# A threshold attention followed by a mixture of attention experts: the opening's loads reordered, and the first pair of heads computed one head at a time

## The chip, the core and the metric

One core of a Trainium2 chip. The metric is the device time of the whole program in microseconds (us), the median over runs. Engines: PE (TensorE, matmuls and transposes), DVE (VectorE), ACT (ScalarE), POOL (GpSimd) and SP (SyncE, which here only issues DMAs). ACT issues DMAs too. PE writes its results to PSUM, eight banks of 512 fp32 columns in 128 partitions; DVE and ACT read them from there.

## The reference

Two stages, in fp32, for batch 8. First an attention with 8 heads, 576 tokens and head size 64, in which only scores within `tau` of their row's maximum count; then, on its output `x` (576 tokens by 512), a mixture of 4 causal attention experts of head size 64, of which each token takes the two with the largest gate.

```python
scores = q @ k.T / sqrt(64)
scores = where(scores >= max(scores) - tau, scores, -1e9)
attn = exp(scores - max(scores)); attn /= sum(attn) + 1e-9
x = attn @ v                              # heads side by side
logits = x @ w_gate                       # top 2 of 4, softmax over them: w
for e in range(4):
    a = softmax(causal(x @ wq[e] @ (x @ wk[e]).T / sqrt(64)))
    out += chosen(e) * w(e) * (a @ (x @ wv[e]) @ wo[e])
```

## The kernel before

The unit of the first stage is a pair of heads: 32 pairs, `pair(n)` for n from 0 to 31, four to a batch. The two heads of a pair lie in partitions 0 to 63 and 64 to 127. `prep(n)` loads the pair and transposes it; 512 of the 576 tokens go as four blocks of 128 (tiles s = 0 to 3), the last 64 tokens of both heads together are a fifth tile (s = 4), loaded into a tile `tm` ("tails": keys and queries). `scores(n, s, qk)` makes a tile: the score matmuls into PSUM (two halves of 288 columns for each head), then for each head DVE's row maximum (`reduce`), POOL's threshold (`thr`), ACT's exponential (`exp`), DVE's masked product with the row sum (`stt`), DVE's addition and reciprocal of the sums (`inverse`), and POOL's multiplication by them (`scaled` on `pp`). `transp` transposes the normalised rows by PE and copies them by ACT, `transp_tails` does it for the last 64 columns, `attnv` multiplies by the values. After the four pairs of a batch, `moe(b)` does the second stage (`projected`, `values`, `scores2`, `transp2`, `attnv2`, `output`), its work mixed with that of the next batch's pairs. Its weights are loaded and split in two parts during the opening (`load_weights`: ACT copies, POOL subtracts).

Pairs 0 and 1 (`DIRECT = 2`) open the kernel, and `first(n)` prepares them without the split into two parts that later pairs have: keys into `ki`, queries into `qi` (in the trace they are `pt`, after the buffer that they use), PE transposes them, ACT copies the keys into `kx` (a `p2` buffer, in the trace `p`), DVE scales the queries into `qx`. Pair 0's tail queries `qd` use an `st` buffer, pair 1's a `pt2t` buffer. In `scores`, the four matmuls of a tile of these pairs (two heads by two halves) are issued with the heads in turn, on partitions 0 to 63 and 64 to 127, and their two bank pairs are taken as one group (`both[-1].v.first = both[0].v`). Each such fp32 matmul is two instructions in the trace: 16 of them are two tiles of two heads.

No engine's order follows the program text. Every operation becomes an `Op` of a `Plan` with a place: a base (the pair, or a number below zero for the opening) plus the number that `PLACE` has for its unit (`"tT"`, or `"tT@0"` for base 0 alone), plus `PLACE_OP` for its engine and tile. `arrange()` runs through planned time: each engine takes, of what is ready by the planned costs and for which buffers are free, what has the smallest sum; PE may start at most `AHEAD = 3` groups beyond the first that is not yet started in its own sorted line. The result is one fixed order on each engine. Every engine's queue, and SP's and ACT's DMA issues in it, is served in that order on the chip; an instruction that waits holds back all behind it. `fill()` puts matmuls with the constant tile `still` into the gaps that the plan shows on PE in the first 80 us; they keep TensorE's clock up and compute nothing that is used. All helpers record their operations in a few lines: L584 a matmul, L1264 a transpose (and every later `fn` of the plan), L1261 a `still` matmul, L605 ACT's copy, L612 a memset, L634 `scaled`, L642 `reduce`, L645 the reciprocal, L656 `stt`, L672 `exp`, L684 a load.

Of the kernel before, what the change touches and what calls it, by code (L numbers as in the profile page):

```python
# [69 lines left out]
}  # L70
# [17 lines left out]
}  # L88
AV_GROUPS = ((4, 0, 1), (2, 3))
AHEAD = 3  # L90
DIRECT = 2
AV2_GROUPS = ((4, 3), (2, 1, 0))
AV2_AT = (((1, "av1"), (2, "av0")), ((2, "av1"), (3, "av1")))

# [1200 lines left out]
```

## Time and profile before

| | |
|---|---|
| median of 3 runs | 924.8 us (924.16 to 925.0) |
| the profiled execution | 924.31 us, of which the span from the first to the last instruction is 922.6 us |
| granted TensorE clock, mean over the span | 0.996 of 2.4 GHz |
| busy share of the span | PE 97%, DVE 80%, ACT 71%, POOL 48% |

Busy shares are means over the span, and PE's contains the `still` matmuls. The rows of a timeline tell when an instruction began, how long it and those merged with it took, how long its engine had been idle before, and what released it.

### The profile page before, as it was taken

To read this page: it belongs to the slowest core of one execution; us is meant where nothing else is said; L and a number is where in the kernel's file an instruction comes from. 1 tells how busy PE (TensorE), PEld (TensorE's weight loads), DVE (VectorE), ACT (ScalarE), POOL (GpSimd) and SP (SyncE) were. 2 spreads that over 40 slices of the span, in tenths; PEclk is the share of its full clock that TensorE was granted. 3 is DMA by queue.
4 is the path that set the end of the run, shared out by engine and by line. 5 is a ranking of instruction groups with operands and counts; after the bars stand their busy time and mean duration, and the time that the engine had idled before them with its cause. 6 is when DMAs were issued, how large, how long until landed. Compare 5 with 4: busy or idle time off the path is not lost.

```text
span 922.6 us, 26089 instructions
## 1 busy us (share of the span) xinstructions
PE 899.3 (97%) x9261; PEld 838.2 (91%) x9261; DVE 736.8 (80%) x2142; ACT 652.4 (71%) x1540; POOL 438.5 (48%) x899
## 2 busy tenths in 40 slices
PE   6899999999999999999999999999999999999996
PEld 5678999899999999999999999999999999999985
DVE  4888879887788869888698877988778886988275
ACT  3678758886778757887587865888677875787453
POOL 4776435554356534555255643555435653444100
PEclk9999999999999999999999999999999999999999
DMA  6544654653755545755437555474474555560151
GB/s 133 143 119 105 154 128 107 159 132 97 173 130 138 140 113 137 178 137 131 120 96 185 125 125 143 116 176 121 102 176 120 145 137 124 123 166 27 50 124 58
DMA packets 147506, 117.86 MB, mean 128 GB/s; under 512 B 98992, under 2 KB 107184, under 8 KB 147376
## 3 DMA queue, kind: packets, MB, share of 16 engines
q1 hardware_dynamic: 144832, 115.61, 51.0%
q8 instruction: 73, 1.20, 0.6%
q10 hardware_dynamic: 2544, 0.59, 0.4%
q14 instruction: 57, 0.47, 0.2%
HBM read 30.42 MB, written 9.44 MB: 43 GB/s over the span
## 4 chain that ended last, share of the span: by engine, by line
PE 86%; DVE 5%; DMA 2%; ACT 2%; POOL 2%; SPq 2%; issue 1%; POOLq 0%; DVEq 0%; ACTq 0%
PE banks L584 64%; PE banks L1264 22%; DVE pp L656 2%; SPq L682 1%; POOL pp L634 1%; ACT pp L672 1%; DVE col L642 1%; DVE banks L661 1%; ACT pt L605 1%; DMA tm<-in_k_dram 1%; SPq L684 1%; DMA pt<-in_k_dram 1%; DVE col L632 0%; DMA st<-in_moe_wq_dram 0%; DMA kt<-hl 0%
## 5 line engine op out<-in xcount | busy, mean ns | idle before, releaser
L634 POOL TENSOR_SCALAR pp<-pp,col 128x576 f32<-128x576 f32 x288 | 212.9, 748 | 177.4 <-DVE col L645 140.3
L642 DVE TENSOR_REDUCE col<-banks 128x1 f32<-128x576 f32 x304 | 226.5, 751 | 35.0 <-PE banks L584 30.8
L656 DVE SCALAR_TENSOR_TENSOR pp<-banks,col,pp 128x576 f32<-128x576 f32 x288 | 231.0, 813 | 29.0 <-ACT pp L672 19.6
L605 ACT ACTIVATE pt<-banks 128x512 f32<-128x512 f32 (+2 forms) x400 | 224.0, 588 | 39.1 <-PE banks L1264 36.6
L672 ACT ACTIVATE pp<-banks,col 128x576 f32<-128x576 f32 (+1 forms) x298 | 217.0, 738 | 42.5 <-DVE col L642 38.0
L1264 PE MATMUL banks<-ident,pp 128*128 128x128 f32 x1342 | 195.7, 275 | 3.3 <-POOL pp L634 1.6
L584 PE MATMUL banks<-kt,qt 128*128 128x288 f32 x960 | 175.3, 311 | 0.9 <-DMA kt<-hl 0.3
L1264 PEld LDWEIGHTS banks<-ident,pp 128*128 128x128 f32 x1342 | 156.5, 141 | 15.0 <-issue 4.1
L634 POOL TENSOR_SCALAR col<-col,tau_n 128x1 f32<-128x1 f32 x288 | 76.7, 268 | 193.5 <-DVE col L642 147.1
L584 PE MATMUL banks<-pt,vm 128*64 128x128 f32 (+1 forms) x2560 | 154.8, 264 | 0.0
L584 PEld LDWEIGHTS banks<-kt,qt 128*128 128x128 f32 x960 | 135.2, 189 | 6.7 <-issue 3.6
L584 PEld LDWEIGHTS banks<-pt,vm 128*64 128x64 f32 x2560 | 131.1, 137 | 8.4 <-issue 4.5
L672 ACT ACTIVATE p<-banks,col 128x576 f32<-128x576 f32 (+4 forms) x134 | 73.2, 553 | 26.3 <-DVE col L661 13.0
L605 ACT ACTIVATE x<-banks 128x256 fp32r<-128x256 f32 (+1 forms) x96 | 28.4, 329 | 73.8 <-PE banks L584 73.7
L634 POOL TENSOR_SCALAR p<-p,col,gw 128x384 f32<-128x384 f32 (+3 forms) x112 | 67.4, 611 | 12.1 <-DVE col L645 6.8
L584 PE MATMUL banks<-wvh,x 128*128 128x260 f32 x320 | 64.3, 285 | 0.0
L661 DVE CUSTOM_DVE_ANT_0 banks<-banks,mask 128x512 f32<-128x512 f32 (+3 forms) x128 | 61.7, 501 | 1.1
L1264 PE MATMUL banks<-ident,p 128*128 128x128 f32 x370 | 57.7, 275 | 2.9 <-DVE p L634 2.7
L616 DVE TENSOR_TENSOR x<-banks,x 128x256 fp32r<-128x256 f32 (+1 forms) x96 | 31.8, 353 | 35.5 <-ACT x L605 34.0
L584 PE MATMUL banks<-ptt,vtz 128*64 128x128 f32 (+1 forms) x640 | 58.9, 262 | 0.0
L632 DVE TENSOR_SCALAR col<-col 128x2 f32<-128x2 f32 (+1 forms) x240 | 47.5, 202 | 11.1 <-ACT p L672 6.7
L584 PE MATMUL banks<-x,wqh 128*128 128x288 f32 x256 | 54.3, 304 | 0.1
(129 smaller groups left out, 1531.0 us busy)
## 6 DMA issues: line engine op xcount, KB each, us to landing
kt<-hl SPq DMA_DIRECT2D x240, 144.0 KB, 2.6
k2x<-q SPq DMA_DIRECT2D x128, 128.0 KB, 2.4
qt<-hl SPq DMA_DIRECT2D x120, 128.0 KB, 2.4
vm<-in_v_dram SPq DMA_DIRECT2D x32, 256.0 KB, 3.1
q2x<-q SPq DMA_DIRECT2D x64, 128.0 KB, 2.3
qi<-in_q_dram SPq DMA_DIRECT2D x60, 128.0 KB, 2.5
ki<-in_k_dram SPq DMA_DIRECT2D x60, 128.0 KB, 3.0
out_dram<-st SPq DMA_DIRECT2D x30, 256.0 KB, 2.5
```

Source lines behind the costliest of these rows:

```text
L584: lambda o, x, y: nc.tensor.matmul(o, x, y, start=start, stop=stop))
L605: run(e, t, [dst], [src], lambda d, s: nc.scalar.activation(d, s, AF.Copy))
L616: lambda d, a, b: (nc.vector if e == "DVE" else nc.gpsimd).tensor_tensor(d, a, b, op=op))
L632: m.tensor_scalar(d, s, x_, None, op0=op0)
L634: m.tensor_scalar(d, s, x_, y_, op0=op0, op1=op1)
L642: lambda d, s: nc.vector.tensor_reduce(d, s, axis=axis, op=op, **({"negate": True} if negate else {})))
L656: nc.vector.scalar_tensor_tensor(d, a_, x_, r.pop(0), op0=op0, op1=op1, **kw)
L661: lambda o, a, i, m: nc.vector.tensor_tensor_reduce(o, i, m, 1.0, 3e38, ALU.add, ALU.min, a))
L672: nc.scalar.activation(d, s, AF.Exp, scale=scale, **kw)
L682: fn = lambda d, s: q_.dma_start(d.bitcast(F32), s.bitcast(F32))
L684: fn = lambda d: q_.dma_start(d, src)
L1264: o.fn(*(r.place() for r in (*o.outs, *o.ins)))
```

## The change

In `first(n)`, the loads of pair 0 get places of their own: the tau load at -36, its keys on SP at -30, its queries on ACT at -29, its tails at -22. The loads of pair 1 are all issued by SP, its queries and tails under units of their own (`qload`, `tload`), and their planned extra latencies are 100 ns instead of 500 and 800. The copy of the transposed keys is split in columns 0 to 287 and 288 to 511, the scaling of the queries in 0 to 127 and 128 to 511.

In the planner, a DMA does not start before the eighth DMA before it has landed (`landed`), an issue on ACT or with an extra latency is charged 650 ns, and the `scaled`, `stt` and `exp` functions return their instruction (nothing uses it).

With `SINGLE = 1`, in pair 0 each head of a score tile is a group of its own in the plan (units `s00` and `s01` instead of `s00` for both), its two matmuls follow each other, and the addition, the reciprocal and POOL's multiplication follow for each head by itself. The matmul's planned cost there is 486 ns instead of 243. For the four pairs of the first batch, tile 4 takes a `p2` or a `pp` buffer, of half the former width.

In `values`, the two memsets come after the matmuls in the text, tied to `v2`'s first operation. Most numbers of `PLACE` for bases 0 to 3 are new, and some of the others.

```diff
-    "tT": -0.5024, "tT@0": -1.2289, "tT@1": -1.9864, "tT@2": -2.326, "tT@3": -2.3822, "tload": -2.4336,
+    "tT": -0.5068, "tT@0": -68.9997, "tT@1": -14.1311, "tT@2": -14.2368, "tT@3": -8.0915, "tload": -2.4336,
...
-    "s00@3": -0.522, "s01": -0.0862, "s01@0": 2.989, "s01@1": -0.4996, "s01@2": -1.2741, "s01@3": -0.1228,
+    "s00@3": -1.4538, "s01": -0.0862, "s01@0": -12.1234, "s01@1": -10.4873, "s01@2": -6.7336, "s01@3": -0.5503,
...
-    "Ls02": 2.2596, "Ls03": 1.9327, "Ls04": 2.2886, "Ls10": 3.1694, "Ls11": 4.41, "Ls12": 2.8143, "Ls13": 3.8614,
+    "Ls02": 2.2596, "Ls03": 1.9327, "Ls04": 2.2886, "Ls10": 3.1694, "Ls11": 4.3918, "Ls12": 2.8143, "Ls13": 3.6877,
...
+SINGLE = 1
...
+            if ops[g].dma:
+                t = max(t, landed[-8])
+                landed.append(t + ops[g].late)
             at[g] = t
...
-            t, more = (243 if x.shape[0] == 64 else 486), 400
+            t, more = (243 if x.shape[0] == 64 and not plan.place[0] < SINGLE else 486), 400
...
-        busy = 580 if e == "SP" else 100
+        busy = 580 if e == "SP" and more == 0 else 650
...
+        plan.ops[-1].dma = True
...
-    plan.place = (-9.45, "load")
-    dma(tau_t, bass.AP(tensor=tau.tensor, offset=tau.offset, ap=[[0, P], [1, 1]]), "ACT")
+    plan.place = (-36.0, "load")
+    dma(tau_t, bass.AP(tensor=tau.tensor, offset=tau.offset, ap=[[0, P], [1, 1]]), "ACT", 1)
...
     def first(n):
-        plan.place = (n / 10 - 9.5, "load")
...
+        plan.place = (n if n else -30.0, "load")
         for j in range(2):
-            dma(ki[:, :, j], ks[:, :, j], "SP", 500)
-            dma(qi[:, :, j], qs[:, :, j], "ACT", 800)
-        dma(tl[ST:], k[0, hs, SM:, :].rearrange("h s d -> s h d"))
-        dma(tl[:ST], q[0, hs, SM:, :].rearrange("h s d -> s h d"), "ACT")
+            dma(ki[:, :, j], ks[:, :, j], "SP", 100)
+        plan.place = (n if n else -29.0, "qload" if n else "load")
+        for j in range(2):
+            dma(qi[:, :, j], qs[:, :, j], "SP" if n else "ACT", 100)
+        plan.place = (n if n else -22.0, "tload" if n else "load")
+        dma(tl[ST:], k[0, hs, SM:, :].rearrange("h s d -> s h d"), "SP", 100)
+        dma(tl[:ST], q[0, hs, SM:, :].rearrange("h s d -> s h d"), "SP" if n else "ACT", 100)
...
-                copy("ACT", kx[:, ST:ST + SM], g)
+                for a, e in ((0, HS), (HS, SM)):
+                    copy("ACT", kx[:, ST + a:ST + e], g[:, a:e])
             else:
-                scaled("DVE", qx[:, :SM], g, qsc, 0.0, ALU.mult, ALU.add)
+                for a, e in ((0, P), (P, SM)):
+                    scaled("DVE", qx[:, a:e], g[:, a:e], qsc, 0.0, ALU.mult, ALU.add)
...
-        pp = plan.tile(("pp", "v2") if n < NPAIR else "pp", [P, 2 * S], F32)
+        pp = plan.tile(("pp", "v2") if n < NPAIR and s < R else ("p2", "pp") if n < NPAIR else "pp", [P, 2 * S if s < R else S], F32)
...
+            alone = n < SINGLE
             both = [plan.tile("s", [P, 2, 512], F32) for _ in range(nj)]
-            both[-1].v.first = both[0].v
-            for hf in range(2):
-                for j in range(nj):
+            if not alone:
+                both[-1].v.first = both[0].v
+            for hf, j in [(hf, j) for j in range(nj) for hf in range(2)] if alone else [(hf, j) for hf in range(2) for j in range(nj)]:
+                if True:
+                    plan.place = (n, f"s{s}{j if alone else 0}")
...
-        inverse(ss[:, :nj])
-        for h in range(nj):
+            if n < SINGLE:
+                inverse(ss[:, js])
+                p = pp[:, j * S:(j + 1) * S]
+                scaled("POOL", p, p, ss[:, js], 0.0, ALU.mult, ALU.add)
+        if n >= SINGLE:
+            inverse(ss[:, :nj])
+        for h in range(nj if n >= SINGLE else 0):
...
-        memset("DVE", v2[:ST, R], 0.0)
-        memset("DVE", lg[:ST, R], 0.0)
...
+        begun = v2.v.ops[0]
+        for x in (v2, lg):
+            memset("DVE", x[:ST, R], 0.0)
+            plan.ops[-1].pre.add(begun)
```

## Rows read from the trace of the kernel before

**Rows 1.** The page, part 1: busy time of each engine, share of the span, instructions.

```profile
PE 899.3 (97%) x9261; PEld 838.2 (91%) x9261; DVE 736.8 (80%) x2142; ACT 652.4 (71%) x1540; POOL 438.5 (48%) x899
```

**Rows 2.** Stages: start:end, length; busy PE, PEld, DVE, ACT, POOL; clock; DMA share, GB/s.

```profile
15.00:20.00 5.00, 3.68 (x13) 3.03 (x14) 3.94 (x11) 2.20 (x4) 2.79 (x7) 0.67 0.31 67
...
30.00:40.00 10.00, 9.87 (x104) 8.53 (x105) 6.38 (x17) 5.99 (x14) 6.57 (x16) 0.83 0.79 191
...
10.93:60.00 49.07, 40.04 (x322) 31.01 (x320) 37.95 (x95) 31.81 (x65) 33.13 (x67) 0.93 0.47 114
...
60.00:100.00 40.00, 38.96 (x481) 36.23 (x482) 35.69 (x92) 30.90 (x64) 24.24 (x53) 1.00 0.56 139
100.00:860.00 760.00, 757.53 (x7949) 716.22 (x7947) 627.65 (x1833) 560.74 (x1328) 377.23 (x759) 1.00 0.53 131
860.00:922.60 62.60, 54.36 (x473) 48.55 (x468) 33.17 (x114) 26.82 (x82) 0.00 (x0) 0.99 0.32 85
```

**Rows 3.** Timeline, first 14 us: start, length, instruction, idle before and its releaser.

```profile
0.80 1.66 SPq L684 DMA_DIRECT2D tm<-in_k_dram  x2
...
2.24 0.61 ACTq L684 DMA_DIRECT2D tau_t<-in_tau_dram  x1
...
2.50 2.67 SPq L684 DMA_DIRECT2D pt<-in_k_dram  x4
...
3.01 1.40 ACTq L684 DMA_DIRECT2D pt<-in_q_dram  x2
...
7.46 0.63 PE L1264 MATMUL banks<-ident,pt 128*128 128x128 f32 x4 [0.85 <-DMA pt<-in_k_dram]
...
8.15 0.60 PE L1264 MATMUL banks<-ident,pt 128*128 128x128 f32 x4
...
8.79 0.75 DVE L634 TENSOR_SCALAR pt<-banks,qsc 128x512 f32<-128x512 f32 x1 [2.09 <-PE banks L1264]
...
9.69 2.21 PE L584 MATMUL banks<-p,pt 64*128 64x288 f32 x16 [0.49 <-DVE pt L634]
...
10.93 2.08 DVE L642 TENSOR_REDUCE col<-banks 128x1 f32<-128x576 f32 x3 [1.39 <-PE banks L584]
```

**Rows 4.** Timeline from 13 to 60 us.

```profile
14.29 0.42 ACT L605 ACTIVATE wqh<-st 128x256 fp32r<-128x256 f32 x1 [5.56 <-POOL st L634]
...
15.44 0.82 DVE L656 SCALAR_TENSOR_TENSOR pp<-banks,col,pp 128x576 f32<-128x576 f32 x1 [2.43 <-ACT pp L672]
...
16.32 1.98 PE L584 MATMUL banks<-p,st 128*128 128x288 f32 x4 [4.43 <-DVE pp L656]
...
18.10 1.06 PE L1264 MATMUL banks<-ident,ki 128*128 128x128 f32 x4
...
18.95 1.06 PE L1264 MATMUL banks<-ident,pt 128*128 128x128 f32 x4
...
24.15 0.60 PE L1264 MATMUL banks<-ident,pp 128*128 128x128 f32 x4
```

**Rows 5.** Timeline of PE from 40 to 62 us.

```profile
41.41 1.24 PE L584 MATMUL banks<-p,pt2t 128*128 128x288 f32 x4
...
51.34 1.24 PE L584 MATMUL banks<-p,pt 64*128 64x288 f32 x8
```

**Rows 6.** Stages, instructions that touch the tile `still` alone.

```profile
20.00:30.00 10.00, 2.53 (x21) 1.99 (x20) 0.00 (x0) 1.00 0.59 143
```

**Rows 7.** Groups of DVE's instructions, first 60 us: busy us, mean ns, idle before.

```profile
L656 DVE SCALAR_TENSOR_TENSOR pp<-banks,col,pp 128x576 f32<-128x576 f32 x20 | 15.6, 814 | 5.2 <-ACT pp L672 3.8 <-ACT pt L605 0.7 <-POOL col L634 0.7
L642 DVE TENSOR_REDUCE col<-banks 128x1 f32<-128x576 f32 x21 | 15.1, 748 | 5.9 <-PE banks L584 5.4 <-ACT pp L672 0.5
...
L645 DVE RECIPROCAL col<-col 128x2 f32<-128x2 f32 (+1 forms) x11 | 1.6, 157 | 0.1
...
L634 DVE TENSOR_SCALAR st<-banks,qsc 64x64 f32<-64x64 f32 x2 | 0.6, 284 | 0.0
...
L612 DVE MEMSET v<- 64x256 f32 x1 | 0.3, 272 | 0.0
```

More of the change, by code (lines that the diff above doesn't have):

```diff
@@ L39 @@
     "Mt030": 1.978, "Mt031": 2.2151, "Mt040": 1.7697, "Mt041": 1.501, "Mt100": 3.9614, "Mt101": 4.9917,
[1 row of a table removed]
[1 row of a table added]
     "Mt140": 3.1832, "Mt141": 3.0207, "Mv0": 1.1833, "Mv1": 0.9428, "Mv2": 1.2052, "Mv3": 0.8227, "Mv4": 0.8632,
[28 rows of a table removed]
[28 rows of a table added]
 }
 PLACE_OP = {
-    "ACT gw": -1.321, "ACT hl": -2.1489, "ACT lg": 0.5171, "ACT p2": -0.0353, "ACT pp": -0.1309, "ACT pt": 0.5826,
-    "ACT ptt": -0.0387, "ACT q2": 1.488, "ACT q2d0": 4.5817, "ACT q2d1": 1.7694, "ACT tau_t": -0.2988,
+    "ACT gw": -1.321, "ACT hl": -2.1489, "ACT lg": 0.5171, "ACT p2": -0.0353, "ACT pp": 0.2646, "ACT pt": 0.4696,
+    "ACT ptt": -0.0387, "ACT q2": 1.5521, "ACT q2d0": 4.5817, "ACT q2d1": 1.7694, "ACT tau_t": -0.3336,
     "ACT tm": -1.4854, "ACT v2": 1.2109, "ACT warm": -1.1366, "ACT wkh": 0.8714, "ACT woh": 1.1122,
@@ L76 @@
     "DVE col": 0.6337, "DVE g": -1.4561, "DVE gate": -1.9949, "DVE gt": -3.3295, "DVE gw": 0.1335,
-    "DVE hl": -3.6827, "DVE lg": 2.0741, "DVE p2": 0.0604, "DVE pp": -0.9317, "DVE pt": -0.5423,
-    "DVE pt2t": 1.7323, "DVE q2": 0.9341, "DVE qsc": -0.1751, "DVE s": -0.5422, "DVE st": -1.8452,
+    "DVE hl": -3.6827, "DVE lg": 2.0741, "DVE p2": 0.0604, "DVE pp": -1.4122, "DVE pt": -0.5423,
+    "DVE pt2t": 1.7323, "DVE q2": 0.9391, "DVE qsc": -0.1751, "DVE s": -0.5422, "DVE st": -1.8452,
     "DVE still": -0.1359, "DVE tau_n": -1.4713, "DVE v2": -0.8112, "DVE warm": -2.9831, "DVE x": 0.2785,
-    "DVE z0": -0.7041, "DVE z1": -2.1009, "DVE zt": 0.323, "POOL col": 0.0444, "POOL hl": 1.1227,
+    "DVE z0": -0.7041, "DVE z1": -2.1009, "DVE zt": 0.323, "POOL col": 0.0444, "POOL hl": 1.0723,
     "POOL ident": -1.4208, "POOL mask": -3.3156, "POOL mask2": -1.1591, "POOL p2": 0.2278, "POOL pp": 1.6676,
@@ L155, in __init__ @@
         self.pre = set()
+        self.dma = False
 def size(x):
@@ L325, in arrange @@
         free = [900.0, 870.0, 800.0, 800.0, 800.0]
+        landed = [0.0] * 8
         ready, future, wake = [[] for _ in engines], [[] for _ in engines], []
@@ L631, in fn @@
             if op1 is None:
-                m.tensor_scalar(d, s, x_, None, op0=op0)
-            else:
-                m.tensor_scalar(d, s, x_, y_, op0=op0, op1=op1)
+                return m.tensor_scalar(d, s, x_, None, op0=op0)
+            return m.tensor_scalar(d, s, x_, y_, op0=op0, op1=op1)
         run(e, t, [dst], [src, *xs], fn)
@@ L655, in fn @@
             x_ = r.pop(0) if kx else x
-            nc.vector.scalar_tensor_tensor(d, a_, x_, r.pop(0), op0=op0, op1=op1, **kw)
+            return nc.vector.scalar_tensor_tensor(d, a_, x_, r.pop(0), op0=op0, op1=op1, **kw)
         run("DVE", cost("DVE", size(dst), True, True), [dst] + ([accum] if accum is not None else []), refs, fn)
@@ L671, in fn @@
                 kw["bias"] = r.pop(0)
-            nc.scalar.activation(d, s, AF.Exp, scale=scale, **kw)
+            return nc.scalar.activation(d, s, AF.Exp, scale=scale, **kw)
         run("ACT", cost("ACT", n, inps(src), accum is not None) + 80, [dst] + ([accum] if accum is not None else []),
@@ L908, in scores @@
         for j in range(nj):
-            plan.place = (n, f"s{s}{j if n >= DIRECT else 0}")
+            plan.place = (n, f"s{s}{j if n >= DIRECT or n < SINGLE else 0}")
             sp = plan.tile("s", [P, 2, 512], F32) if n >= DIRECT else both[j]
```

70 rows, old and new, of tables (PLACE, PLACE_OP) are left out of this document.

## The prediction

> **What bounds the kernel now.** I read the page first. TensorE (PE) is busy for 97% of the span [rows 1]. A busy PE can also be a PE that only multiplies the constant tile `still` to keep its clock, so I next cut the span into stages and looked for what PE did not do in each [rows 2]. In the middle, from 100 to 860 us, PE is busy 757.5 of 760 us: 2.5 us are idle there, and no new order of work can win more than that. From 60 to 100 us it is 38.96 of 40. The last 62.6 us have 8.2 us of idle time. The first 60 us are different: VectorE (DVE) is at work for 37.95 of the 49.07 us after its first row maximum, 77%, while PE is slowed by its clock (granted 0.67 of 2.4 GHz on average in 15 to 20 us, 0.83 in 30 to 40) and fills holes with `still`: 2.53 us of it between 20 and 30 us alone [rows 2, 6]. So what the change can move is the opening, and a gain there reaches the end almost whole, because PE has no idle time in which a lead could get lost before 860 us.
>
> Then the opening instruction by instruction. The order is: both pairs' tails are issued first on SP and ACT, tau third on ACT, the keys from 2.50 us on SP, the queries from 3.01 us on ACT. PE transposes the first pair's keys at 7.46 and its queries at 8.15; DVE scales the queries (0.75 us) and the first scores start at 9.69 [rows 3]. Sixteen instructions, that is two query tiles for both heads, fill all eight banks by 11.9. DVE takes three maxima from 10.93 to 13.0. The reader is to see what comes next: ScalarE (ACT) does not start the exponentials, it stands at the copy of a weight, `wqh`, until 14.29, since that weight's tile has landed late; its exponentials follow it on the same queue. DVE idles 2.43 us before its first masked product at 15.44, and PE, which has no bank, 4.43 us, until 16.32. After that idle time PE's next four score instructions take 1.98 us [rows 4]; four of the same shape take 1.24 us later, at the full clock [rows 5].
>
> **The change part by part.** *The loads.* The tau load is placed first on ACT, then keys on SP and queries on ACT, then the tails of the first pair; everything of pair 1 goes to SP behind them. The second key load was issued at 2.50 + 0.67 = 3.17 and its transposes began 4.3 us later. It will now be issued at 0.80 + 0.83 = 1.6 (the first issues on SP took 0.83 each), so about 5.9. The second query load was issued at 3.01 + 0.70 = 3.71, the transposes started 4.4 us later; now it is third on ACT, at 0.8 + 0.61 + 0.70 = 2.1, so about 6.5, 1.65 us sooner. The query scaling comes in pieces of 128 and 384 columns; by the line through 0.75 us for 512 and 0.28 us for 64 columns [rows 3, 7] they cost 0.35 and 0.62, so the first scores can start 0.4 us sooner. Together 2.05 us; I take 2.0: first maximum at about 8.9. The bound on the other side is the tail: `tT@0` has the first place in PE's line (-69), and its query half is now fourth on ACT, issued at 2.8; at the same 4.4 us it lands at 7.2, and the gain is 1.0. With the whole split and no queue it is 2.4.
>
> Pair 1's queries and tail leave ACT for SP: three issues of 0.67 us, 2.0 us of SP's queue. Behind them stand pair 2's loads and the weights. I cost it at nothing because the next loads are first used at 18.10 (pair 2's keys) and 18.95 (a `pt` tile of pair 1) at present [rows 4], after the wait for a bank; without that cover it is 2.0 us.
>
> *The planned semaphores.* The planner now lets every load wait for the landing of the eighth before it, and charges 650 instead of 100 ns for an issue on ACT. Nothing of this is run on the chip; it changes in which order the queues stand. What it should remove is the weight copy in front of the first exponentials: the 2.43 us that DVE idled. The bounds are 0 (another late thing takes its place) and 2.43.
>
> *The clock.* With that hole gone, PE does not wait 4.43 us for a bank. What the clock cost is, from the stages, 3.68 x (1 - 0.67) = 1.2 us and 9.87 x (1 - 0.83) = 1.7 us [rows 2]. Part of that PE time was `still`, and DVE was busy 64 to 79% in these stretches and set part of the pace. I take 1.0 of the 2.9; the bounds are 0 and 2.9.
>
> *Head by head.* Now a score tile of pair 0 belongs to one head, takes two banks, and is normalised on its own. For DVE this adds one addition and one reciprocal (0.15 us each, row of the reciprocal [rows 7]) in four tiles: 1.2 us. With 0.2 us for the split queries and 0.3 us saved by the memset of the moe values (0.27 us [rows 7]), which leaves the opening, DVE gets 1.1 us more work: +1.1, between 0.8 and 1.4. ACT's split of the keys costs one more fixed part, under 0.2 us, while ACT is idle.
>
> For PE the change takes something away. Eight instructions on 64 partitions, the two heads in turn, take 1.24 us at full clock; four on 128 partitions take 1.24 too [rows 5]. So the two heads now run at once. In the new order four instructions of one head follow each other, in one half of the array. The trace has no such run; per head the bounds are 0.62 (it would still overlap) and 1.24. I take 1.24, since four instructions on one set of rows are nearest to the four on all rows: 0.62 x 8 heads = 5.0 us more PE time in pair 0. The Trainium skill says the same: in "TensorEngine Tiling (Array Packing)", section "Tiling Modes", different tiles of the array can run matmuls in parallel, so that giving up the pairing doubles the time; the trace agrees, 1.24 us for eight against 1.24 for four, and by that rule the sum below would be 5.0 us worse if PE set the pace. On the path I count 0 of these 5.0 us: half lies in the 4.43 us in which PE waited, half in the 2.53 us of `still`, and one head per 1.24 us is still faster than DVE, which needs 0.75 + 0.81 us for it [rows 7]. If that cover is gone all 5.0 count. What is gained in return, banks that are free one head sooner and the first normalised rows to transpose long before the present 24.15 [rows 4], is what lets DVE go on without a gap; I price it only by the gaps named above.
>
> *The new places elsewhere* (moe, the last batch) meet a PE without idle time; I take 0, between a win of 1.5 us out of the last stage's 8.2 and the loss of one wait as large as the 2.4 or 4.4 us that DVE and PE stood in the opening [rows 4].
>
> Sum: -2.0 - 2.4 - 1.0 + 1.1 = -4.3 us. The profiled execution took 924.31 us (span 922.6 and 1.7 around it); that gives 920.0. The median of the three runs is 924.8, 0.5 above, so **920.5 us**.
>
> **The rivals.** *DVE never waits.* If it runs from 8.9 us at the share that it has from 60 to 100 us, 35.69/40 = 89% [rows 2], its 37.95 + 1.1 = 39.05 us are done 43.8 us later, at 52.7 instead of 60: 7.3 us, 917.5. For it: one head per bank pair, and work for PE early. Against it: 60 to 100 us has the moe to choose from, the opening only four pairs.
>
> *The lead is given back.* The earlier start is real (-2.0) and so is the added work (+1.1), but a weight or pair 2's load again stands before the exponentials or the copies and the order reached is no denser: -0.9, 923.9, which is no change here. For it: SP has three issues more, and POOL and ACT still split all weights in the same 60 us (POOL is busy 6.57 and ACT 5.99 of 10 us from 30 to 40 [rows 2]).
>
> *Slower: PE sets the pace in pair 0.* Without the pairing PE needs 5.0 us more; it decides if PE is busy with real work without a break from the first score to 60 us. Then -2.0 + 5.0 = +3.0, 927.8. For it: PE is busy 9.87 of 10 us from 30 to 40 already. Against it: part of that is `still` and half clock, and the doubled work lies before 25 us.
>
> **How the numbers follow.** A change under 0.2% (1.85 us) can't be told from none. Forecast, 918 to 922.9: 0.52. DVE never waits, under 918: 0.20. Given back, within 0.2%: 0.14. Slower: 0.14. So faster 0.72, same 0.14, slower 0.14. The range reaches from 916 (the 917.5 with the 1.5 us from the last stage) to 927, most of the way to the slower case; I leave out about 0.05 below and 0.1 above. The likeliest's own range is 918 to 922.9.
>
> **What would show it.** Right: the first maximum between 8.5 and 9.9 us; the first exponential within 1 us of it, no weight copy before it; no PE wait over 3 us after the first score; granted clock near 1.0 from 15 to 20 us; the first transposes of `pp` before 20 us; score instructions of pair 0 at 1.24 us per head; DVE share from its first maximum to 60 us at 83% or more; 100 to 860 us as it is now. Wrong: a PE that stands at the tail transposes with keys and queries landed, a weight copy that stands before exponentials at another place, or new idle time after 60 us.

## The result, and the profile of the changed kernel

The changed kernel takes 930.46 us (median of four, 929.57 to 933.1) against 924.48 for the kernel before beside it: a ratio of 1.0071, 95% interval 1.0048 to 1.0094. It is slower by some 6 us; the forecast was 920.5.

The page of the changed kernel, first part, and the row of the granted clock from its second part (tenths of full speed, 40 slices of 23 us). All line numbers of the changed kernel are higher by five or more: L590 is a matmul, L1285 a transpose, L1282 a `still` matmul.

```profile
PE 903.9 (97%) x9213; PEld 841.1 (91%) x9213; DVE 735.6 (79%) x2152; ACT 652.7 (70%) x1542; POOL 438.8 (47%) x899
...
PEclk8799799999999999999999999999999999999999
```

DVE and ACT did about as much as before [rows 1]. PE was busy 4.6 us longer, with 48 instructions fewer (there are 48 `still` matmuls fewer, as will be seen), and its clock was lower in the opening and once more in the fifth slice, about 93 to 116 us. The stages (columns as in [rows 2]):

```profile
10.00:15.00 5.00, 3.86 (x21) 2.43 (x18) 4.75 (x12) 2.51 (x4) 1.03 (x4) 1.00 0.81 205
15.00:20.00 5.00, 4.42 (x10) 2.69 (x11) 4.00 (x15) 0.87 (x2) 5.00 (x11) 0.57 0.14 25
20.00:25.00 5.00, 3.31 (x11) 2.22 (x11) 3.49 (x8) 3.46 (x7) 1.93 (x6) 0.50 0.62 145
25.00:30.00 5.00, 5.00 (x14) 2.86 (x14) 2.47 (x12) 1.51 (x3) 2.30 (x5) 0.50 0.56 136
30.00:40.00 10.00, 9.14 (x50) 6.44 (x48) 8.76 (x24) 7.92 (x16) 8.08 (x17) 0.86 0.45 125
...
60.00:100.00 40.00, 37.39 (x465) 34.28 (x464) 30.08 (x78) 29.50 (x63) 22.25 (x48) 1.00 0.45 110
100.00:860.00 760.00, 755.02 (x7905) 716.24 (x7905) 627.14 (x1831) 557.13 (x1319) 374.23 (x755) 0.99 0.54 132
```

Three things are to be seen. DVE starts well: 4.75 of 5 us from 10 to 15. Then PE falls to 1.2 GHz: 0.57 on the mean of 15 to 20 us is 4.3 of 5 us at half speed, 0.86 of 30 to 40 is 2.8 of 10, so from about 15.7 to 32.8 us. And from 60 to 100 us, where no part of the opening is left, DVE does 30.08 us of work instead of 35.69 [rows 2].

The opening itself, from the timeline of the first 24 us (columns as in [rows 3]):

```profile
6.28 0.63 PE L1285 MATMUL banks<-ident,pt 128*128 128x128 f32 x4 [0.46 <-DMA pt<-in_q_dram]
...
7.01 0.62 PE L1285 MATMUL banks<-ident,pt 128*128 128x128 f32 x4
...
8.71 3.15 PE L590 MATMUL banks<-p,pt 64*128 64x288 f32 x16 [0.75 <-DVE p L613]
...
9.96 0.76 DVE L647 TENSOR_REDUCE col<-banks 128x1 f32<-128x576 f32 x1 [1.26 <-PE banks L590]
...
10.75 0.74 ACT L677 ACTIVATE pp<-banks,col 128x576 f32<-128x576 f32 x1 [2.42 <-DVE col L647]
...
12.60 1.23 PE L590 MATMUL banks<-p,pt 64*128 64x288 f32 x4 [0.74 <-DVE pp L661]
...
15.59 2.19 PE L590 MATMUL banks<-p,pt 64*128 64x288 f32 x4 [0.82 <-DVE pp L661]
...
17.57 0.42 ACT L611 ACTIVATE wqh<-st 128x256 fp32r<-128x256 f32 x1 [2.12 <-POOL st L639]
```

The first exponential follows the first maximum after 0.79 us and the copy of `wqh` stands behind it at 17.57 us, no longer in front. One head (four instructions in one half of the array) takes 1.23 us at the full clock, and 2.19 once it has fallen. The first normalised rows are transposed at 26.13 us, 2 us later than before [rows 4], not sooner.

**Where the lead goes.** Adding up DVE's busy time is a simple ledger, since both kernels give DVE nearly the same work. The sums of all windows up to 60 us are 40.30 us before and 43.61 after: 3.3 us ahead. The next two windows of the kernel before, and then of the changed one:

```profile
60.00:80.00 20.00, 19.15 (x246) 17.71 (x246) 17.78 (x49) 14.92 (x33) 14.30 (x32) 1.00 0.53 134
80.00:100.00 20.00, 19.81 (x237) 18.52 (x237) 17.90 (x43) 15.98 (x33) 9.94 (x22) 1.00 0.59 144
```

```profile
60.00:80.00 20.00, 19.66 (x238) 17.72 (x238) 18.40 (x49) 16.96 (x35) 11.32 (x24) 1.00 0.34 82
80.00:100.00 20.00, 17.72 (x232) 16.56 (x228) 11.68 (x32) 12.53 (x29) 10.93 (x25) 1.00 0.56 137
100.00:120.00 20.00, 17.16 (x130) 16.52 (x132) 13.52 (x34) 11.43 (x25) 9.00 (x20) 0.74 0.53 132
```

At 80 us DVE is 3.9 us ahead (62.01 against 58.08), at 100 us 2.3 behind (73.69 against 75.98). So 6.2 us are lost between 80 and 100 us. DVE's timeline of the changed kernel says on what:

```profile
87.95 0.95 DVE L622 TENSOR_TENSOR hl<-banks,hl 128x512 fp32r<-128x512 f32 x2 [0.77 <-ACT hl L611]
92.62 0.42 DVE L622 TENSOR_TENSOR x<-banks,x 128x256 fp32r<-128x256 f32 x1 [3.73 <-ACT x L611]
95.51 0.56 DVE L622 TENSOR_TENSOR x<-banks,x 128x256 fp32r<-128x256 f32 x2 [2.46 <-ACT x L611]
95.98 0.75 DVE L647 TENSOR_REDUCE col<-banks 128x1 f32<-128x576 f32 x1
```

There are no scores to reduce from 87 to 96 us: pair 3's are done and pair 4's have not come. PE's timeline shows the two sides. First the kernel before, where pair 4's scores (`kt,qt`) lie between pair 3's transposes and values, then the changed one:

```profile
88.49 0.78 PE L584 MATMUL banks<-kt,qt 128*128 128x288 f32 x4
...
93.50 0.77 PE L584 MATMUL banks<-kt,qt 128*128 128x288 f32 x4
...
100.05 0.39 PE L584 MATMUL banks<-ptt,vtz 128*64 128x128 f32 x4
...
104.30 0.53 PE L584 MATMUL banks<-x,wkh 128*128 128x288 f32 x2
```

```profile
94.45 0.48 PE L590 MATMUL banks<-ptt,vtz 128*64 128x128 f32 x4
94.87 0.79 PE L590 MATMUL banks<-kt,qt 128*128 128x288 f32 x4
...
99.91 0.66 PE L1285 MATMUL banks<-ident,qi 128*128 128x128 f32 x4 [2.28 <-POOL qi L639]
...
105.93 1.97 PE L1285 MATMUL banks<-ident,pp 128*128 128x128 f32 x8 [2.84 <-DVE col L647]
107.55 0.83 PE L590 MATMUL banks<-x,wkh 128*128 128x288 f32 x2
```

Pair 3's values end on PE at 94.9 us instead of 100.4, but pair 4's first scores come at 94.87 instead of 88.49. PE has them alone then, with nothing to mix them with: it stands 2.28 us for pair 5's queries and 2.84 us for pair 4's rows, its clock falls again (0.74 on the mean of 100 to 120 us: 10.4 us at half speed), and the first `moe` matmul comes 3.25 us later than before. The first output leaves at 199.88 us instead of 193.74, 6.1 later; from there to the end it is 728.5 us against 728.9. All that the change costs has been lost by then. In every kernel below, this last stretch is 728.0 to 730.1 us, so the time of the first output tells each profiled execution.

What pair 4 waits for is its place on PE, not its loads. The last part of its queries is loaded at 52.21 us and scaled by POOL at 56.8, its keys are loaded from 62.65. PE transposes them only at 85.21 and 86.52 (before: 81.86 and 82.30), without an idle moment in front; then SP copies the two parts of queries and keys into `qt` and `kt`, until 94.56:

```profile
85.21 0.60 PE L1285 MATMUL banks<-ident,qi 128*128 128x128 f32 x4
86.48 2.42 SPq L687 DMA_DIRECT2D qt<-hl  x4
86.52 0.60 PE L1285 MATMUL banks<-ident,ki 128*128 128x128 f32 x4
88.95 5.61 SPq L687 DMA_DIRECT2D kt<-hl  x8
```

### The profile page after: what moved, and what is told of

Read it like the earlier page. It is cut to its first block, busy times and chain, and to the rows that moved or that the text cites. A ratio compares the mean times of both kernels' runs of the same rounds, so it can differ in the third digit from the quotient of the medians.

```text
span 928.4 us, 26030 instructions
## 1 busy us (share of the span) xinstructions
PE 903.9 (97%) x9213; PEld 841.1 (91%) x9213; DVE 735.6 (79%) x2152; ACT 652.7 (70%) x1542; POOL 438.8 (47%) x899
## 4 chain that ended last, share of the span: by engine, by line
PE 77%; DVE 9%; ACT 6%; SPq 3%; issue 2%; DMA 2%; POOL 0%; ACTq 0%; DVEq 0%
PE banks L590 58%; PE banks L1285 19%; SPq L687 3%; DVE pp L661 2%; ACT pp L677 2%; DVE col L647 1%; ACT p L677 1%; ACT pt L611 1%; DVE banks L666 1%; DVE gt L613 1%; DMA kt<-hl 1%; DVE q L622 1%; DMA k2x<-q 0%; DMA pt<-in_q_dram 0%; DVE gw L622 0%
## 5 line engine op out<-in xcount | busy, mean ns | idle before, releaser
L639 POOL TENSOR_SCALAR pp<-pp,col 128x576 f32<-128x576 f32 x278 | 205.4, 748 | 172.0 <-DVE col L650 132.1
L661 DVE SCALAR_TENSOR_TENSOR pp<-banks,col,pp 128x576 f32<-128x576 f32 x278 | 223.5, 813 | 26.5 <-ACT pp L677 16.1
L677 ACT ACTIVATE pp<-banks,col 128x576 f32<-128x576 f32 (+1 forms) x289 | 210.6, 737 | 41.4 <-DVE col L647 35.9
L1285 PE MATMUL banks<-ident,pp 128*128 128x128 f32 x1296 | 191.4, 276 | 7.5 <-DVE pp L639 4.0
L590 PE MATMUL banks<-kt,qt 128*128 128x288 f32 x960 | 176.8, 312 | 1.2 <-DMA kt<-hl 0.5
L1285 PEld LDWEIGHTS banks<-ident,pp 128*128 128x128 f32 x1296 | 152.4, 142 | 20.1 <-issue 5.4
L590 PE MATMUL banks<-pt,vm 128*64 128x128 f32 (+1 forms) x2560 | 155.0, 264 | 0.0
L590 PEld LDWEIGHTS banks<-kt,qt 128*128 128x128 f32 x960 | 136.9, 190 | 8.2 <-issue 3.9
L590 PEld LDWEIGHTS banks<-pt,vm 128*64 128x64 f32 x2560 | 131.4, 137 | 8.1 <-issue 3.9
L677 ACT ACTIVATE p<-banks,col 128x256 f32<-128x256 f32 (+4 forms) x137 | 75.7, 560 | 32.3 <-DVE col L666 17.2
L590 PE MATMUL banks<-wvh,x 128*128 128x260 f32 x320 | 64.3, 285 | 0.0
L1285 PE MATMUL banks<-ident,p 128*128 128x128 f32 x389 | 60.9, 275 | 0.6 <-ACT pt L611 0.5
L590 PE MATMUL banks<-ptt,vtz 128*64 128x128 f32 (+1 forms) x640 | 59.3, 262 | 0.0
L590 PE MATMUL banks<-k2x,q2x 128*128 128x256 f32 (+3 forms) x256 | 54.1, 335 | 1.3 <-DMA k2x<-q 0.3
```

The lines of the kernel that those rows point to most:

```text
L590: lambda o, x, y: nc.tensor.matmul(o, x, y, start=start, stop=stop))
L639: return m.tensor_scalar(d, s, x_, y_, op0=op0, op1=op1)
L661: return nc.vector.scalar_tensor_tensor(d, a_, x_, r.pop(0), op0=op0, op1=op1, **kw)
L677: return nc.scalar.activation(d, s, AF.Exp, scale=scale, **kw)
L1285: o.fn(*(r.place() for r in (*o.outs, *o.ins)))
```

## The experiments

Each ratio is to the kernel before, run beside it on the same chip (its medians there: 924.61 for the first four kernels, 924.35 for the next four, 925.52 for the last four). The ratio and its interval are those of the record; the quotient of the two medians differs from it by up to 0.0012. The first output's time is from the profiled execution.

| kernel | median us | ratio, 95% interval | first output at us |
|---|---|---|---|
| e1_side | 927.88 | 1.0047 (1.0028 to 1.0066) | 196.27 |
| e2_queue | 929.64 | 1.0056 (1.0040 to 1.0072) | 198.46 |
| e3_both | 927.78 | 1.0040 (1.0025 to 1.0055) | 197.23 |
| b_nostill | 924.70 | 0.9994 (0.9976 to 1.0011) | 193.94 |
| e6_four | 922.24 | 0.9973 (0.9959 to 0.9987) | 189.78 |
| e7_fourside | 921.25 | 0.9977 (0.9958 to 0.9996) | 189.64 |
| p_loads | 923.72 | 0.9992 (0.9978 to 1.0006) | 193.38 |
| p_single | 930.67 | 1.0079 (1.0060 to 1.0098) | 198.70 |
| e8_only4 | 923.25 | 0.9976 (0.9962 to 0.9990) | 193.65 |
| e8_onlyw | 933.06 | 1.0082 (1.0063 to 1.0101) | 200.63 |
| p_singleside | 934.27 | 1.0101 (1.0072 to 1.0131) | 201.51 |
| b_four | 922.45 | 0.9963 (0.9948 to 0.9979) | 191.17 |

### Is it the clock? e1_side and b_nostill

The `still` matmuls of the changed kernel, and of the one before (shortest, median and longest in ns, first and last start in us):

```profile
L1282 PE MATMUL banks<-still x25: 272/421/421, 1.2 to 7.7; 128*128 128x256 bf16 x25
```

```profile
L1261 PE MATMUL banks<-still x73: 272/273/421, 1.2 to 50.0; 128*128 128x256 bf16 x73
```

`fill()` puts a `still` only where a whole bank is free. Head by head, scores hold all eight from 8.7 us on, and there are no more `still`s. e1_side is the changed kernel with 70 `still`s more, up to 40 us; where no bank is free they write columns 304 to 495 of a score tile's bank, of which the scores use 288. They compute nothing that is used.

```diff
-            if n > (0 if t < cold else 3):
+            if n > (0 if t < dense else 3):
...
+                else:
+                    for bank in range(8):
+                        if all(f == "s" or y + 150.0 < t or x > a for x, y, f in used[bank]):
+                            res += [(t + 20.0 + i * w, bank + 8) for i in range(n)]
+                            break
...
+                o_ = banks[:, n, :256] if n < 8 else banks[:, n - 8, 304:496]
```

> The changed kernel with 70 more matmuls of the constant tile in PE's planned gaps up to 40 us; no bank is free there, so they write 192 columns that a score tile leaves unused in its banks. Order of all else as before. Theory 'clock' (the 17 us at 1.2 GHz from 15.7 to 32.8 us are what the change lost): granted clock 2.4 GHz up to 40 us, and 4 to 7 us less, 923 to 926 us. Theory 'queue' (what was lost was lost at 97 to 106 us, where PE stands for pair 4's loads): the opening gets faster, but the lead is swallowed at 100 us; at most 1.5 us less, 929 us or more.

The clock is 1.00 in all windows up to 100 us, DVE is 6.2 us ahead at 80 us (64.23 against 58.08), and of the 6 us only 2.6 come back: 927.88, between the two theories. PE's timeline of e1_side:

```profile
91.61 0.48 PE L595 MATMUL banks<-ptt,vtz 128*64 128x128 f32 x4
92.02 0.79 PE L595 MATMUL banks<-kt,qt 128*128 128x288 f32 x4
...
97.49 0.66 PE L1291 MATMUL banks<-ident,qi 128*128 128x128 f32 x4 [1.95 <-POOL qi L644]
...
103.41 1.97 PE L1291 MATMUL banks<-ident,pp 128*128 128x128 f32 x8 [3.48 <-POOL pp L644]
105.03 0.83 PE L595 MATMUL banks<-x,wkh 128*128 128x288 f32 x2
```

Pairs 0 to 3 now end 8.3 us sooner than before, and again pair 4 comes only behind them, with the same two stalls, 5.4 us together. So the clock of the opening is not the whole loss. How large a part it is, this run doesn't tell: its fillers wait for readers themselves (3.3 us from 16 to 60 us), and the second fall of the clock is not gone but smaller, 0.91 from 100 to 120 us.

The mean granted clock of every execution is on record, and within one kernel the time follows it. The kernel before, beside the last four kernels, took 922.68 to 925.03 us in four executions at 0.996 and 927.04 to 928.22 in four at 0.991. The changed kernel's four have 0.983 to 0.988. If the clock costs as much there, which no run shows, the 0.008 by which its median lies below that of the kernel before would alone be worth its whole loss (an estimate from these executions). But at an equal clock of 0.996 e1_side's three executions took 927.47 to 928.15, the kernel before's five beside it 922.06 to 924.63: with the stalls at pair 4 and the fillers' waits, and without the low clock, 4 to 5 us are lost.

The other way round, the kernel before with its `still`s only up to 9 us (43 of 73 left out):

```diff
-    idle = plan.fill(1250.0, 80000.0, 9000.0, 110.0, 217.0)
+    idle = plan.fill(1250.0, 9000.0, 9000.0, 110.0, 217.0)
```

> The kernel before, without its 43 matmuls of the constant tile between 9 and 80 us (of 73); nothing else is changed. Theory 'clock': TensorE stays at 1.2 GHz for 10 us or more in the first 60 us, as in the changed kernel, and the time rises by 3 to 6 us, 927.5 to 930.5. Theory 'queue': the opening is paced by VectorE, so PE's clock costs at most 1 us there: 924 to 925.5.

924.70 us, no difference, as the theory 'queue' said. Without them its clock is 0.83 in 10 to 20 and in 20 to 30 us, 3.4 us at half speed each, and not 17: in that order PE's own work keeps the clock up for most of the time. So missing `still`s alone don't slow the old order down; only together with the new order do they go with 17 us at half speed.

### Is it a queue? e2_queue and e3_both

In the changed kernel a weight load (`st` from `wv`) stood on SP in front of pair 4's loads, waiting for POOL's `wkl`. The waits of SP from 60 to 110 us:

```profile
SPq L689 <- POOL wkl L622: 11.9, 2, 11.6
```

e2_queue moves the copy and the subtraction of that weight forward in the finished order, so that the buffer is free sooner; nothing else moves. e3_both is this and the `still`s of e1_side.

```diff
     order = plan.arrange()
+    plan.when[next(n for n, o in enumerate(plan.ops) if o.kind == 'ACT wkh' and o.unit == 'w2')] = 67300.0
+    plan.when[next(n for n, o in enumerate(plan.ops) if o.kind == 'POOL wkl' and o.unit == 'w2')] = 68200.0
+    order.sort(key=lambda n: (plan.when[n], n))
```

> The changed kernel with two instructions moved forward in the fixed order: the copy of the weight part wk of chunk 2 on ACT and its subtraction on POOL come right behind the landing of that part (near 75 us instead of 78.8 and 84.1), so that SP's next weight load, which needs their buffer, does not hold SP's queue until 84.87 us. Theory 'queue': SP goes on at about 76 us, PE's waits of 2.28 and 2.84 us at 97.6 and 103 us go and with them the second stretch at 1.2 GHz; 5 to 9 us less, 921 to 925 us. Theory 'clock': the waits at 100 us only reflect a late opening; at most 2 us less, 928 us or more.

> Both edits together. If the two losses are separate, their gains add: 917 to 921 us, below the kernel before. If there is one loss, this run is no faster than the better of the two.

929.64 and 927.78 us: the same as without it, within the intervals, and so no gain of 5 to 9 us. The wait of 11.6 us is gone, and another has its place:

```profile
SPq L689 <- PE banks L590: 14.2, 4, 8.5
```

The next load in the queue needs a value buffer that PE has still to read. And PE's order is as it was: pair 4's transposes come at 85.29 and 86.60 us, its copies on SP from 86.55 to 94.48, the stalls are 1.83 and 3.47 us. So this wait alone did not hold pair 4 back. That the queue plays no part is not shown, since the edit didn't make pair 4's copies come sooner; what is left is pair 4's place.

### Is it pair 4's place? e6_four, e7_fourside, e8_only4 and e8_onlyw

Pair 4 is the first whose numbers in `PLACE` the change left nearly alone: it has the general ones, of which five are new (`load` went from -4.5178 to -4.6245), and none of those for its scores and for the transposes of its keys and queries. e6_four is the changed kernel with places of its own for pair 4 (loads, transposes and scores earlier) and other ones for the four weight loads; e7_fourside has the `still`s of e1_side too; e8_only4 has pair 4's numbers alone, e8_onlyw those of the weights alone.

```diff
+PLACE.update({"w0": -1.4346, "w1": -5.0149, "w2": 1.4859, "w3": 2.1572,
+    "kT@4": -2.1368, "qT@4": -1.6095, "tT@4": -2.1203, "load@4": -4.7856, "qload@4": -1.701, "tload@4": -3.373,
+    "s00@4": -0.0518, "s01@4": -0.1832, "s10@4": -0.2406, "s11@4": -0.0218, "s20@4": 0.5519,
...
+    "av0@4": 1.1081})
```

> The changed kernel with other places for pair 4 alone (its loads, transposes and scores earlier in the plan) and for the weight loads; the planned order up to 53 us is that of the changed kernel but for two weight loads. Theory 'pair 4' (the changed kernel has pairs 0 to 3 done earlier, but pair 4, whose places did not move, comes no sooner, and PE stands between them): PE's waits of 2.3 and 2.8 us near 100 us go, and the time falls by 4 to 7 us, to 923.5 to 926.5, since the slow clock in the opening stays. Theory 'clock': the waits near 100 us are paid elsewhere; 928.5 us or more.

> The same with the matmuls of the constant tile in the score tiles' unused columns up to 40 us as well. Theory 'pair 4': now the lead that the clock cost comes through to the end: 2 to 4 us less than without them, 920 to 924 us, below the kernel before. Theory 'clock': the opening's clock alone, 926 to 928 us.

> The changed kernel with the other places of pair 4 alone; the weight loads keep the change's places. Theory 'pair 4': nearly all of the 8 us that the run with both gave, 922 to 924 us, and no PE wait over 1 us from 90 to 110 us. Theory 'weights' (it was the weight load that held SP's queue until 84.87 us): less than half of it, 926.5 us or more.

> The changed kernel with the other places of the weight loads alone. Theory 'weights': 926 us or less. Theory 'pair 4': no gain, 929 us or more; its own plan is 2.2 us longer than the change's.

With pair 4's places the changed kernel is faster than the one before, 0.9973 and 0.9976 (e6_four's 922.24 us are a little below its forecast); with the weights' places alone it stays slow, 1.0082. In e8_only4 pair 4's keys and queries are transposed at 77.74 and 79.94 us, 8.8 and 5.3 us sooner than in the changed kernel, and its scores follow 5.1 us sooner:

```profile
77.74 0.61 PE L1286 MATMUL banks<-ident,ki 128*128 128x128 f32 x4
79.94 0.66 PE L1286 MATMUL banks<-ident,qi 128*128 128x128 f32 x4 [0.68 <-DVE v L662]
89.75 0.77 PE L591 MATMUL banks<-kt,qt 128*128 128x288 f32 x4
```

No wait of PE from 90 to 110 us is over 0.21 us there, as forecast, and the clock is 1.00 from 100 to 120 us: with the stalls, the second fall of the clock is gone too. PE's timeline of e6_four:

```profile
88.06 0.77 PE L591 MATMUL banks<-kt,qt 128*128 128x288 f32 x4
...
97.14 0.39 PE L591 MATMUL banks<-ptt,vtz 128*64 128x128 f32 x4
...
99.38 0.51 PE L591 MATMUL banks<-x,wkh 128*128 128x288 f32 x2
```

Pair 4's scores begin at 88.06, 9.5 us before pair 3's values end, PE stands nowhere from 80 to 120 us (20.00 of 20 in both windows), and `moe` begins 8.2 us sooner than in the changed kernel. The `still`s of e7_fourside add nothing that can be measured on top (0.9977), where 2 to 4 us were forecast. e8_only4 keeps the low clock of the opening (0.76, 0.50 and 0.88 in the three 10 us from 10 to 40 us) and its median is below that of the kernel before all the same; its profiled execution, 924.8 us, is one of its slowest, so that its first output (193.65) shows no gain. DVE does only 13.66 us of work from 80 to 100 us in it, against 17.90 in the kernel before, while PE is busy for 19.63: a gap in DVE's ledger alone is no loss, as long as PE has other work in it.

### Which half of the change? p_loads, p_single and p_singleside

p_loads is the kernel before with the new opening loads alone: their order, pair 1's on SP with the new places, and the split copies (as in the change; the diff shows some of it). p_single is the kernel before with the first pair head by head alone, its places near the old ones, and the half-width buffers of tile 4 that come with it; p_singleside has the `still`s of e1_side too.

```diff
+PLACE.update({"load@1": -21.1286, "qload@1": -21.3467, "tload@1": -20.479})
...
+    plan.place = (-36.0, "load")
...
+        plan.place = (n if n else -30.0, "load")
```

```diff
+PLACE.update({"s00@0": -1.3, "s01@0": -1.28, "s10@0": -1.2281, "s11@0": -1.2081,
+    "s20@0": -1.0493, "s21@0": -1.0293, "s30@0": -0.5811, "s31@0": -0.5611})
+SINGLE = 1
```

> The kernel before with one part of the change alone: the order of the opening's loads, all of pair 1's on SP, and the two split copies (places of pair 1's three load units as in the change; tau first). The prediction's first term: the first row maximum comes 2 us sooner and the end with it, 922 to 923.5 us. Theory 'pair 4', that what comes after sets the end: the first maximum is sooner, but the second stage of the batch begins when it did, 924 to 925.5 us.

> The kernel before with another part alone: pair 0 head by head, its heads next to each other in the order (tile 0's first place moved from -163.9 to -1.3, since the old order can't be kept). The prediction's count: its PE time is hidden, 924 to 926 us. The prediction's slower rival, 5.0 us more PE time on the path: 928 to 930 us. Its own plan is 2.9 us longer than that of the kernel before, so 927 to 928 would be the plan's doing.

> The kernel before with pair 0 head by head alone, as measured at 930.7 us, and with matmuls of the constant tile in unused columns of the score tiles up to 40 us, where no bank is free for them. If the lost clock (13.7 us at 1.2 GHz from 15.4 us) is what the head-by-head part costs: 926 to 927.5 us, its plan's own 2.9 us left. If it is PE's added 5 us of matmul time or the wait for banks: 929 us or more.

The loads do nothing that can be told from none: 0.9992. Yet this run has the gains that the prediction added up: the first maximum comes at 9.65 us, 1.3 sooner, the copy of `wqh` stands behind three exponentials (14.86 us), the clock is 1.00 up to 40 us, and at 20 us DVE is 4.3 us ahead (12.65 against 8.38). By 60 us it has done 39.37 us of work against 40.30, and the first `moe` matmul comes at 104.29 us instead of 104.30: by DVE's sums, the lead is given back within the opening here, before pair 4 plays a part. Head by head alone, in this order, costs as much as the whole change: 1.0079, 930.67 us, nearest to the slower rival's 928 to 930. Its plan was 2.9 us longer by itself, so not all of this need be the matmuls' doing. The windows from 20 us on of p_single:

```profile
20.00:30.00 10.00, 9.35 (x34) 6.40 (x32) 5.81 (x19) 4.29 (x8) 5.40 (x11) 0.55 0.38 92
...
80.00:100.00 20.00, 17.52 (x198) 16.38 (x198) 15.65 (x38) 14.35 (x29) 10.52 (x22) 1.00 0.54 131
```

PE is busy 9.35 of 10 us from 20 to 30 with 34 instructions (63 before, 21 of them `still` [rows 6]) at little over half the clock. At 80 us DVE is 0.5 us behind, at 100 us 2.7; PE stands 2.35 us for pair 3's rows at 88.1. p_singleside was to take the clock away from this and doesn't: the clock is 1.00 from 20 us on, but the `still`s in this order wait for the readers of the bank that they write in, and it took 934.27 us. Its waits of PE in the first 130 us (sum, times, longest; L1277 is the `still`):

```profile
PE banks L1277 <- DVE pp L663: 3.7, 4, 1.0
PE banks L1277 <- ACT pp L679: 3.0, 4, 0.9
```

So this run says nothing on the clock's share; it stays open.

### The same repair without the change: b_four

The kernel before, with pair 4's places looked for in the same way:

```diff
+PLACE.update({"w3": 3.1635, "s21@4": 0.7803, "perm@4": 1.3099, "t40@4": 0.5034,
+    "tload@4": -2.0959, "t20@4": 0.9666, "s31@4": 0.9047})
```

> The kernel before, with new places for pair 4 (and one weight chunk) alone, searched for in the same way as for the changed kernel; its plan is 2.5 us shorter than before's. If pair 4's place was a cause of its own in the changed kernel, because the opening there ran ahead of it, there is little to win here: 922.5 to 925. If better places for pair 4 are worth as much to any opening: 4 us or more, 920.5 or less, and the change's opening itself is worth nothing.

922.45 us, 0.9963 (0.9948 to 0.9979), 3.1 us below the kernel before beside it: between the two theories, and as fast as the best of the changed ones. PE is busy 20.00 of 20 us from 100 to 120, where the kernel before had 19.31, and the first `moe` matmul comes at 101.26 us:

```profile
101.26 0.51 PE L585 MATMUL banks<-x,wkh 128*128 128x288 f32 x2
```

What the changed kernel gets below the kernel before with pair 4 moved, the kernel before gets too. The new opening by itself is then worth nothing that these runs can tell. Still, moving pair 4 is worth more to the new opening: the ratio falls by 0.0095 there (1.0071 to 0.9976) and by 0.0037 here, though the places come from two searches. This, e6_four, e7_fourside and e8_only4 are below both kernels; their intervals overlap.

## Why the prediction was wrong

**The step that failed** is the last sentence of its first paragraph: "a gain there reaches the end almost whole, because PE has no idle time in which a lead could get lost before 860 us". That PE had little idle time from 60 to 100 us was true of the old order, in which pair 4 came in time to be mixed with pair 3. A lead of pairs 0 to 3 makes them end sooner; it doesn't make pair 4 come sooner, whose places the change left where they were: its transposes came 3.4 and 4.2 us later than before. The lead was there, 3.9 us of DVE's work at 80 us, and turned into a gap of 6.2 us in the next 20. e8_only4 shows it: the same opening with pair 4 moved takes 0.24% less than the kernel before, not 0.71% more. Even then the lead does not reach the end, since b_four, with the old opening, takes 0.37% less. p_loads says the same without pair 4: 4.3 us ahead at 20 us, and the end unmoved. The prediction named "new idle time after 60 us" as a sign of its being wrong, and never asked what would cause it.

**The loads, -2.0.** Measured -1.0 (first maximum 9.96 against 10.93 [rows 3]), the bound that it gave for the tails. The queries were transposed at 6.28 us, 0.2 sooner than forecast, the keys at 7.01, 1.1 later; the first score then waited for DVE's copy of the tail's keys until 8.71.

**The weight copy, -2.4.** Right in mechanism: `wqh` stands behind the exponentials, the first masked product comes at 11.72 instead of 15.44 [rows 4], and no wait of PE in the first 16 us is over 1.3 us. p_loads has this too, and the end did not move with it.

**The clock, -1.0.** Wrong in sign: 0.57 from 15 to 20 us, where the prediction looked for near 1.0. The prediction took the old `still`s for granted and even booked half of PE's 5.0 us to them, as cover. In the new order no bank is free for them: 25 remain of 73, none after 7.7 us, and the clock was at half speed for 17 us instead of twice about 3.4. Putting it right gave 2.6 us back (e1_side), with fillers that wait themselves for a bank's readers and a second fall, at 100 us, that stays; so the clock may have cost more than that; by the scatter of the executions it could be as much as the loss.

**Head by head on DVE, +1.1.** Over-sized: its part for the heads was 1.2; in p_single, which has that part alone, DVE's busy time is 737.3 us against 736.8 [rows 1], 0.5 more.

**Head by head on PE, 0 of 5.0.** The price was right, 1.23 us for a head. The Trainium skill's rule that was cited ("TensorEngine Tiling (Array Packing)", section "Tiling Modes") agrees for a head that stands alone. Four heads one behind the other took 3.15 us here and 3.00 in p_single, 0.79 and 0.75 each, against 0.55 in pairs (2.21 for four [rows 3]); that is less than four times 1.23, so neighbours in opposite halves still overlap in part. Counting it as hidden was wrong for a stretch: from 25 to 30 us of the changed kernel PE is busy 5.00 of 5 us at half speed while DVE has 2.47. The cover that was named, the `still`s, had gone, and the first normalised rows came to PE at 26.13 us instead of long before 24.15. What it costs in the end is not known; p_single's 0.79% holds its longer plan too. The rival "PE sets the pace in pair 0" (927.8) was right on this stretch and on the sign, but not on the sum: with the clock put right DVE does 8.28 of 10 us from 20 to 30, and the kernel still loses.

**What stays open.** How much of the changed kernel's loss is clock and how much the gap at pair 4, since the second fall of the clock comes with that gap. How p_single's loss divides between the clock, the lost pairing and its fixed order. Pairing both heads inside the changed order with the new places was not tried. Which of pair 4's numbers does the work in e8_only4 was not taken apart, and what took p_loads' lead between 20 and 60 us was not looked for.

## What to carry to other kernels

A lead in an opening is worth what the next stage can take: find the first piece of work whose place does not move, and ask when it arrives and what the engines have to mix it with once the work ahead ends sooner. Adding up the busy time of one engine whose work is the same in both kernels, window by window, shows where to look for a lost lead; whether it is lost, the engine that is always busy decides. Filler work that keeps the clock up needs a place to write to; an order that holds every bank takes it away, and its cost must stand in the sum.

## What the hardware showed that was not expected

The granted clock fell to 1.2 GHz at about 15.7 us and came back at about 32.8, although PE was busy for 4.42, 3.31 and 5.00 us of the three 5-us windows in between; what it did there were single heads on 64 partitions (2.19 us each) and transposes, after `still`s had ended at 7.7 us and after waits of 0.74 and 0.82 us. In the kernel before, without its later `still`s (b_nostill), PE was busy less, 5.66 of 10 us from 10 to 20, and its clock was 0.83 there; the changed kernel was busy for 8.27 of these 10 us at 0.79 (1.00 and 0.57 in the two halves). So the stretch with the larger busy share had the lower clock. Nor is it the same in every execution of one order: e2_queue, whose opening is that of the changed kernel, had 0.83, 0.66 and 0.83 in the three 10 us from 10 to 40 us, the changed kernel 0.79, 0.50 and 0.86.
